# Three staging buffers for a float64 weight conversion, with router operands formed per 128 features

## The chip, the cores and the metric

The program runs on one core of one Trainium2 chip. The metric is the device time of one execution in microseconds (us). Inputs lie in device memory (HBM); the host only re-lays them, without arithmetic. The core has five engines with an in-order queue each: TensorE (PE in the profile, its weight loads PEld), VectorE (DVE), ScalarE (ACT), GpSimd (POOL), and SyncE (SP), which here issues all DMA transfers. An instruction that waits holds up everything behind it on its engine.

## The reference

Three stages in a row on 2304 tokens (4 batches of 576), width 512:

```python
scores = scale * q @ k.T + (cum[:, None] - cum[None, :])   # cum = cumsum(log f); causal
x = softmax(scores) @ v                                     # 8 heads of 64
x = (silu(x @ w_gate) * (x @ w_val)) @ w_out                # d_ff 1536; these weights are float64
P = exp(x @ moe2_w_gate - max)                              # 8 experts, dense
for _ in range(8): P /= P.sum(1); P /= P.sum(0); P *= N / E # balanced over rows and columns
out = sum_e P[:, e] * (relu(x @ w1[e]) @ w2[e])             # 8 experts, inner size 1024
```

The three weights of the middle stage are float64: numpy's draw is scaled by a float64 scalar. The kernel gets them as raw 64-bit words and makes float32 values of them on the chip. All large products are done on a high and a low part of each operand (float32r), three matmuls for one.

## The kernel before, in words

The work is four "units", one for a batch. Unit b is attention of batch b (`attn_unit`, eight heads in four pairs) and the gated feed-forward of batch b (`moe_unit`, six slices of 256 inner features, each in two token blocks of 288). `merge` interleaves attention of batch b+1 with the feed-forward of batch b in program order; a scheduler of the tile framework, which models the engines, then sets each engine's order of instructions. After the fourth unit the second phase starts: the router's balancing and the eight experts.

The float64 weights come in 18 pieces of 1 MB, three for a slice: two of the up-projections, one of the down-projection. `convert(i)` turns piece i into a float32 high and low part:

- SyncE loads the raw words into a tile `st` (line 103). Two such tiles exist, so the load of piece i+2 stands on SyncE's queue behind the end of piece i.
- VectorE masks the exponent word (line 111, into `y`), ScalarE shifts it (113, `y` to `g`), VectorE sets the sign (114), masks (116, into `y` again) and scales the middle word (117, in place in `st`).
- GpSimd adds the two in two halves (122, in `st`). ScalarE copies each half into the high part of a tile `w` (124) and GpSimd forms the low part by `rest` (line 143, a helper: `out = src - hi`).
- SyncE stores `w` to HBM (`wsplit`, 126), whence units 1 to 3 fetch it again (`fetch`, 138).

The `w` tiles are a ring of four. Unit 0 multiplies directly from it, so a piece is written to its `w` only when unit 0 has used up the piece four before it. Line 151 (helper `three`) is every three-part matmul of the feed-forward and of the down-projections of the experts: tile `pm` for the up-projections, `py` for the down-projections. Per slice that is 96 `pm` and 48 `py` matmuls of 288 columns in a unit, 144 for three pieces.

In attention, `qk` and `cb` are the loads of a head (232, 244), `qkh` and `kl` the split by GpSimd. For batches 2 and 3 a masked copy `cm` of `cb` takes the tiles of tag `st`.

At a unit's end `finish` (from line 446) stores the result `x` and forms the router's products: for each half of the tokens, `x` is split into high and low parts (tile `f`, 128x576 at a time, line 456 on ScalarE, `rest` on GpSimd), multiplied into a PSUM tile `pl` (460; one of three tiles that `pm` and `py` use too), copied to `ls` (464) and stored to `lgd` (465). Pool `frm` holds two `f` tiles and one `ls`.

Of the kernel before, what the change touches and what calls it, by code (L numbers as in the profile page):

```python
# [8 lines left out]
F32 = mybir.dt.float32  # L9
F32R = mybir.dt.float32r  # L10
BF16 = mybir.dt.bfloat16
U16 = mybir.dt.uint16
U32 = mybir.dt.uint32
AF = mybir.ActivationFunctionType
ALU = mybir.AluOpType
# [18 lines left out]
def attention_two_ffns(ctx: ExitStack, tc: tile.TileContext, qkT, vt, f, wf, g2, w1, w2, out):  # L34
    nc = tc.nc
    B, H, D, _, S = qkT.shape
# [4 lines left out]
    P = 128  # L41
    KD = DM // P
# [4 lines left out]
    HP = 512  # L47
# [13 lines left out]
    frm = m_ctx.enter_context(pool("frm", 2))  # L61
# [15 lines left out]
    gw = const.tile([P, KD, P], F32R, name="gw")  # L77
# [5 lines left out]
    HB = S // 2  # L83
# [14 lines left out]
    def convert(i):  # L98
        base = bases[:, 1:2] if i % 3 == 2 else bases[:, 0:1]
        W = 2 * HP  # L100
        st = cvp.tile([P, 4 * W + 4], U16, tag="st", name="st", bufs=2)
        with tc.issue_after(last_qk[0].ins) if i < PACE else ExitStack():
            nc.sync.dma_start(out=st[:, 1:1 + 4 * W], in_=wf[i].bitcast(U16))

        def words(dt):
            return st.bitcast(dt)[:, 0:2 * W].rearrange("p (i t) -> p i t", t=2)[:, :, 1]
        mid, v = words(U32), words(F32)
        top = st[:, 4:4 + 4 * W].rearrange("p (i t) -> p i t", t=4)[:, :, 0]
        y = cvp.tile([P, W], U16, tag="y", name="y")
        g = cvp.tile([P, W], U16, tag="g", name="g")  # L110
        nc.vector.tensor_scalar(out=y, in0=top, scalar1=0x7fff, scalar2=None, op0=ALU.bitwise_and)  # L111

        nc.scalar.activation(out=g, in_=y, func=AF.Relu, scale=8.0, bias=base)
        nc.vector.scalar_tensor_tensor(
            out=g, in0=top, scalar=0x8000, in1=g, op0=ALU.bitwise_and, op1=ALU.bitwise_or)
        nc.vector.tensor_scalar(out=y, in0=g, scalar1=0xff80, scalar2=None, op0=ALU.bitwise_and)
        nc.vector.scalar_tensor_tensor(
            out=v, in0=mid, scalar=2.0**-36, in1=y.bitcast(BF16), op0=ALU.mult, op1=ALU.mult)
        t = wring.tile([P, 2, 2, HP], F32R, tag="w", name="w")
        halves = [slice(j * HP, (j + 1) * HP) for j in range(2)]  # L120
        for h in halves:
            nc.gpsimd.tensor_tensor(out=v[:, h], in0=v[:, h], in1=g[:, h].bitcast(BF16), op=ALU.add)  # L122
        for j, h in enumerate(halves):
            nc.scalar.copy(out=t[:, j, 0], in_=v[:, h])  # L124
            rest(t[:, j, 1], v[:, h], t[:, j, 0])
        nc.sync.dma_start(out=wsplit[i], in_=t.bitcast(F32))
        return t
# [13 lines left out]
    def rest(out, src, hi, eng=None):  # L141

        (eng or nc.gpsimd).tensor_tensor(out=out, in0=src, in1=hi.bitcast(F32), op=ALU.subtract)  # L143
# [13 lines left out]
    cvp = at_ctx.enter_context(pool("cvp", 2, side="right"))  # L157
# [47 lines left out]
    def attn_unit(b):  # L205
# [22 lines left out]
        def load(h):  # L228
            qk = raw.tile([P, 2, S], F32, tag="qk", name="qk")
            src = qkT[b, h]  # L230
# [4 lines left out]
            if r < NPE:  # L235

                for c0 in (0, HB):
                    ps = ps_t.tile([P, 512], F32, tag="t", name="ps_c")
                    nc.tensor.matmul(
                        out=ps[:, 0:HB], lhsT=ident[0:B * H, r:r + 1].to_broadcast([B * H, P]), rhs=ct[:, c0:c0 + HB],  # L240
                        start=True, stop=True)
# [2 lines left out]
                nc.sync.dma_start(out=cb, in_=cumd[r:r + 1, :].to_broadcast([P, S]))  # L244
            cm = None
            if b in MASKED:
                cm = cvp.tile([P, 8 * HP + 4], U16, tag="st", name="cm", bufs=2).bitcast(F32)[:, 0:S]
                nc.gpsimd.tensor_tensor(
                    out=cm[:, 0:512].rearrange("p (t c) -> p t c", c=P), in0=cb[:, 0:512].rearrange("p (t c) -> p t c", c=P),
                    in1=maskf.unsqueeze(1).to_broadcast([P, 4, P]), op=ALU.add)  # L250
                nc.gpsimd.tensor_tensor(out=cm[64:P, 512:S], in0=cb[64:P, 512:S], in1=maskf[64:P, 64:P], op=ALU.add)
# [143 lines left out]
    def moe_unit(b, get=fetch, ready=None):  # L395
# [50 lines left out]
        def finish():  # L446

            x = xa["x"]
            nc.sync.dma_start(out=xd[b], in_=x)
            for j in range(2):  # L450
                tk = slice(j * HB, (j + 1) * HB)
                pl = ps_m.tile([P, 512], F32, tag="m", name="pl")
                for i in range(2):
                    t = frm.tile([P, 2, 2, HB], F32R, tag="f", name="f")
                    src = x[:, 2 * i:2 * i + 2, tk]
                    nc.scalar.copy(out=t[:, 0], in_=src)
                    rest(t[:, 1], src, t[:, 0])
                    ops = [(hl, k) for k in range(2) for hl in range(2)]
                    for n, (hl, k) in enumerate(ops):
                        nc.tensor.matmul(  # L460
                            out=pl[:, 0:HB], lhsT=gw[:, 2 * i + k], rhs=t[:, hl, k],
                            start=(i == 0 and n == 0), stop=(i == 1 and n == len(ops) - 1))
                ls = frm.tile([P, HB], F32, tag="ls", name="ls", bufs=1)
                nc.scalar.copy(out=ls[0:2 * E], in_=pl[0:2 * E, 0:HB])
                nc.sync.dma_start(out=lgd[:, b * S + j * HB:b * S + (j + 1) * HB], in_=ls[0:2 * E])

# [301 lines left out]
```

## Time and profile before

| | |
|---|---|
| runs, median of 3 (lowest to highest) | 2263.25 us (2262.04 to 2266.35) |
| the profiled execution | 2262.41 us |
| its span, first to last instruction | 2260.6 us |
| TensorE busy | 2210.3 us, 98% |
| VectorE, GpSimd, ScalarE busy | 75%, 40%, 38% |
| moved from and to HBM | 193.27 MB read, 36.87 MB written |

A busy share is a mean over stages that differ: conversion runs only in the first 282.4 us, the experts from some 740 us on. So the rows below look at stretches. A "window" row gives for a stretch each engine's busy time and its number of instructions; the stretch's length stands in front. In the "chain of waits" each piece is what released the next, back from the last instruction.

### The profile page before, as it was taken

How to read it: one execution, taken by the hardware profiler on the slowest of the kernel's cores; microseconds unless marked ns; L12 is line 12 of the kernel's file. 1: busy time of each engine (PE TensorE's matmuls, PEld its weight loads, DVE VectorE, ACT ScalarE, POOL GpSimd, SP SyncE). 2: the span in 40 equal slices, each digit the busy share in tenths (PEclk: the TensorE clock that was granted, in tenths of full speed). 3: DMA queues.
4: the chain of work that ended last, by engine and by line, in shares of the span. 5: the costliest groups of instructions: out<-in, count | busy, mean ns of one | idle time of the engine just before them, and what ended most of it. 6: DMA issues, size and time to landing. Idle time of an engine off the chain costs nothing.

```text
span 2260.6 us, 36388 instructions
## 1 busy us (share of the span) xinstructions
PE 2210.3 (98%) x13801; PEld 2013.9 (89%) x13801; DVE 1698.7 (75%) x3513; ACT 852.6 (38%) x1952; POOL 908.8 (40%) x716
## 2 busy tenths in 40 slices
PE   7898799999999999999999999999999999999999
PEld 5698799999999888898898989988989898988997
DVE  7778755656635798887878878877788887887876
ACT  7866464555422434322323223233232232322321
POOL 6869754544523454332323323233232332322320
PEclk9999999999999999999999999999999999999999
DMA  9766566554544332111111111151111111111101
GB/s 251 203 204 218 197 206 194 188 187 149 206 160 154 102 118 87 63 47 38 56 38 47 47 38 53 60 211 54 38 48 47 38 57 38 47 47 38 57 29 52
DMA packets 105103, 232.50 MB, mean 103 GB/s; under 512 B 10672, under 2 KB 60128, under 8 KB 92896
## 3 DMA queue, kind: packets, MB, share of 16 engines
q1 hardware_dynamic: 104928, 230.18, 31.5%
q8 instruction: 108, 1.77, 0.3%
q14 instruction: 67, 0.55, 0.1%
HBM read 193.27 MB, written 36.87 MB: 102 GB/s over the span
## 4 chain that ended last, share of the span: by engine, by line
PE 84%; DMA 6%; DVE 4%; POOL 2%; ACT 1%; issue 1%; SPq 1%; POOLq 0%; DVEq 0%; ACTq 0%
PE py L151 40%; PE pa L614 30%; PE pm L151 10%; DMA st<-wf 3%; PE ps_o L353 2%; PE ps_t L322 1%; DMA rd<-rt 1%; PE ps_s L279 1%; PE ps_s L283 1%; DVE al L629 1%; DMA rb<-rd 1%; DMA qk<-qkT 1%; DVE y L111 0%; DVE sm L580 0%; POOL st L122 0%
## 5 line engine op out<-in xcount | busy, mean ns | idle before, releaser
L614 PE MATMUL pa<-xf,w1h 128*128 128x288 f32 x3584 | 748.7, 295 | 0.2 <-DVE u L623 0.2
L614 PEld LDWEIGHTS pa<-xf,w1h 128*128 128x128 f32 x3584 | 597.6, 188 | 37.8 <-DVE u L623 0.7
L666 DVE SCALAR_TENSOR_TENSOR acc<-py,lg,acc 128x512 f32<-128x512 f32 x531 | 394.8, 744 | 246.6 <-PE py L151 246.4
L614 PE MATMUL pa<-xf,w1l 128*128 128x288 f32 x1792 | 527.6, 295 | 0.0
L143 POOL TENSOR_TENSOR w2l<-w,w2h 128x1024 fp32r<-128x1024 f32 x64 | 154.7, 2418 | 819.2 <-ACT w2h L590 819.2
L151 PE MATMUL py<-w2h,ah 128*128 128x512 f32 x1152 | 454.2, 394 | 1.8 <-DVE acc L659 0.7
L151 PE MATMUL py<-w2l,ah 128*128 128x512 f32 x1152 | 454.0, 394 | 0.0
L151 PE MATMUL py<-w2h,al 128*128 128x512 f32 x1152 | 453.3, 393 | 0.0
L629 DVE SCALAR_TENSOR_TENSOR al<-c,ah 128x288 fp32r<-128x288 f32 x512 | 429.7, 866 | 5.6 <-ACT ah L628 4.9
L628 ACT ACTIVATE ah<-c 128x288 fp32r<-128x288 f32 x512 | 208.2, 443 | 566.3 <-PE py L151 319.0
L614 PEld LDWEIGHTS pa<-xf,w1l 128*128 128x128 f32 x1792 | 337.0, 188 | 10.6
L151 PE MATMUL pm<-xh,w 128*128 128x288 f32 x1536 | 331.2, 300 | 13.6 <-ACT w L124 8.9
L151 PEld LDWEIGHTS pm<-xh,w 128*128 128x128 f32 x1536 | 255.0, 190 | 17.8 <-ACT w L124 10.6
L151 PEld LDWEIGHTS py<-w2h,al 128*128 128x128 f32 x1152 | 216.3, 188 | 50.0
L151 PEld LDWEIGHTS py<-w2h,ah 128*128 128x128 f32 x1152 | 216.3, 188 | 31.0 <-DVE acc L666 2.3
L151 PEld LDWEIGHTS py<-w2l,ah 128*128 128x128 f32 x1152 | 216.3, 188 | 26.2
L151 PE MATMUL pm<-xl,w 128*128 128x288 f32 x768 | 228.0, 297 | 0.5 <-POOL xl L143 0.5
L634 ACT COPY m<-pa 128x288 f32<-128x288 f32 x128 | 50.3, 393 | 435.8 <-PE pa L614 433.6
L143 POOL TENSOR_TENSOR w1l<-w,w1h 128x256 fp32r<-128x256 f32 x192 | 162.2, 872 | 128.7 <-ACT w1h L586 128.7
L151 PE MATMUL py<-ah,w 128*128 128x288 f32 x768 | 174.4, 299 | 4.5 <-DVE xa L444 2.1
L143 POOL TENSOR_TENSOR w1l<-sm,w1h 128x1024 fp32r<-128x1024 f32 x64 | 153.8, 2403 | 2.5 <-ACT w1h L586 2.5
L143 POOL TENSOR_TENSOR al<-th,ah 128x288 fp32r<-128x288 f32 x96 | 82.9, 866 | 160.6 <-ACT ah L428 157.9
(149 smaller groups left out, 3099.4 us busy)
## 6 DMA issues: line engine op xcount, KB each, us to landing
w<-w SPq DMA_DIRECT2D x128, 512.0 KB, 3.6
w<-wsplit SPq DMA_DIRECT2D x54, 1024.0 KB, 5.0
qk<-qkT SPq DMA_DIRECT2D x64, 288.0 KB, 7.1
st<-wf SPq DMA_DIRECT2D x18, 1024.0 KB, 9.8
wsplit<-w SPq DMA_DIRECT2D x18, 1024.0 KB, 4.5
cb<-cumd SPq DMA_DIRECT2D x31, 288.0 KB, 6.1
xo<-h SPq DMA_DIRECT2D x28, 288.0 KB, 2.2
xf<-xo SPq DMA_DIRECT2D x14, 576.0 KB, 11.0
```

What stands on the lines that cost most here:

```text
L143: (eng or nc.gpsimd).tensor_tensor(out=out, in0=src, in1=hi.bitcast(F32), op=ALU.subtract)
L151: nc.tensor.matmul(out=ps, lhsT=a, rhs=b, start=(i == 0), stop=(i == n - 1))
L279: nc.tensor.matmul(out=ps[:, 0:w], lhsT=a[:, qs:qs + P], rhs=kh[:, c0:c0 + w], start=True, stop=False)
L283: nc.tensor.matmul(out=ps[:, 0:w], lhsT=a[:, qs:qs + P], rhs=kl[:, c0:c0 + w], start=False, stop=True)
L322: nc.tensor.transpose(pv[:, j, :], pt[r0:P, k0:k0 + P], ident[r0:P, r0:P])
L353: nc.tensor.matmul(out=po[:, c0:w], lhsT=vs[:, j, e].rearrange("p a d -> p (a d)"), rhs=pts[rng][part][:, j, c0:w], start=(i == 0), stop=( ...
L614: nc.tensor.matmul(out=ps, lhsT=w[:, MW[m - 1], k], rhs=x[:, m - 1, hl, k], start=(n == 0), stop=(n == len(ops) - 1))
L628: nc.scalar.activation(out=ah[:, f, tk], in_=src, func=AF.Relu)
L629: nc.vector.scalar_tensor_tensor(out=al[:, f, tk], in0=src, scalar=0.0, in1=ah[:, f, tk].bitcast(F32), op0=ALU.max, op1=ALU.subtract)
L634: nc.scalar.copy(out=m1, in_=p1)
L666: nc.vector.scalar_tensor_tensor(out=a, in0=py, scalar=lg[:, t, e:e + 1], in1=a, op0=ALU.mult, op1=ALU.add)
```

## The change

The tag `st` gets a third buffer (at both places that use it). The masked exponent word is written to `g` instead of `y`, and ScalarE works on `g` in place; `y` keeps one buffer, `g` gets three. The router operands are formed per 128 features (eight tiles of 128x288 in high and low part for a batch's two halves) instead of per 256; `ls` takes a tile of the same tag `f`, so that `f` and `ls` share two buffers.

```diff
--- before.py
+++ after.py
@@ -98,7 +98,7 @@
     def convert(i):
         base = bases[:, 1:2] if i % 3 == 2 else bases[:, 0:1]
         W = 2 * HP
-        st = cvp.tile([P, 4 * W + 4], U16, tag="st", name="st", bufs=2)
+        st = cvp.tile([P, 4 * W + 4], U16, tag="st", name="st", bufs=3)
         with tc.issue_after(last_qk[0].ins) if i < PACE else ExitStack():
             nc.sync.dma_start(out=st[:, 1:1 + 4 * W], in_=wf[i].bitcast(U16))
 
@@ -106,11 +106,11 @@
             return st.bitcast(dt)[:, 0:2 * W].rearrange("p (i t) -> p i t", t=2)[:, :, 1]
         mid, v = words(U32), words(F32)
         top = st[:, 4:4 + 4 * W].rearrange("p (i t) -> p i t", t=4)[:, :, 0]
-        y = cvp.tile([P, W], U16, tag="y", name="y")
-        g = cvp.tile([P, W], U16, tag="g", name="g")
-        nc.vector.tensor_scalar(out=y, in0=top, scalar1=0x7fff, scalar2=None, op0=ALU.bitwise_and)
-
-        nc.scalar.activation(out=g, in_=y, func=AF.Relu, scale=8.0, bias=base)
+        y = cvp.tile([P, W], U16, tag="y", name="y", bufs=1)
+        g = cvp.tile([P, W], U16, tag="g", name="g", bufs=3)
+        nc.vector.tensor_scalar(out=g, in0=top, scalar1=0x7fff, scalar2=None, op0=ALU.bitwise_and)
+
+        nc.scalar.activation(out=g, in_=g, func=AF.Relu, scale=8.0, bias=base)
         nc.vector.scalar_tensor_tensor(
             out=g, in0=top, scalar=0x8000, in1=g, op0=ALU.bitwise_and, op1=ALU.bitwise_or)
         nc.vector.tensor_scalar(out=y, in0=g, scalar1=0xff80, scalar2=None, op0=ALU.bitwise_and)
@@ -244,7 +244,7 @@
                 nc.sync.dma_start(out=cb, in_=cumd[r:r + 1, :].to_broadcast([P, S]))
             cm = None
             if b in MASKED:
-                cm = cvp.tile([P, 8 * HP + 4], U16, tag="st", name="cm", bufs=2).bitcast(F32)[:, 0:S]
+                cm = cvp.tile([P, 8 * HP + 4], U16, tag="st", name="cm", bufs=3).bitcast(F32)[:, 0:S]
                 nc.gpsimd.tensor_tensor(
                     out=cm[:, 0:512].rearrange("p (t c) -> p t c", c=P), in0=cb[:, 0:512].rearrange("p (t c) -> p t c", c=P),
                     in1=maskf.unsqueeze(1).to_broadcast([P, 4, P]), op=ALU.add)
@@ -450,17 +450,15 @@
             for j in range(2):
                 tk = slice(j * HB, (j + 1) * HB)
                 pl = ps_m.tile([P, 512], F32, tag="m", name="pl")
-                for i in range(2):
-                    t = frm.tile([P, 2, 2, HB], F32R, tag="f", name="f")
-                    src = x[:, 2 * i:2 * i + 2, tk]
-                    nc.scalar.copy(out=t[:, 0], in_=src)
-                    rest(t[:, 1], src, t[:, 0])
-                    ops = [(hl, k) for k in range(2) for hl in range(2)]
-                    for n, (hl, k) in enumerate(ops):
+                for k in range(KD):
+                    t = frm.tile([P, 2, HB], F32R, tag="f", name="f")
+                    nc.scalar.copy(out=t[:, 0], in_=x[:, k, tk])
+                    rest(t[:, 1], x[:, k, tk], t[:, 0])
+                    for hl in range(2):
                         nc.tensor.matmul(
-                            out=pl[:, 0:HB], lhsT=gw[:, 2 * i + k], rhs=t[:, hl, k],
-                            start=(i == 0 and n == 0), stop=(i == 1 and n == len(ops) - 1))
-                ls = frm.tile([P, HB], F32, tag="ls", name="ls", bufs=1)
+                            out=pl[:, 0:HB], lhsT=gw[:, k], rhs=t[:, hl],
+                            start=(k == 0 and hl == 0), stop=(k == KD - 1 and hl == 1))
+                ls = frm.tile([P, 2, HB], F32, tag="f", name="ls")[:, 0]
                 nc.scalar.copy(out=ls[0:2 * E], in_=pl[0:2 * E, 0:HB])
                 nc.sync.dma_start(out=lgd[:, b * S + j * HB:b * S + (j + 1) * HB], in_=ls[0:2 * E])
 
```

The scheduler makes a new order of the whole program from it. On SyncE's queue near its start (names: `st_507`, `st_776`, `st_1062` are pieces 1, 2 and 3; `cb` and `qk` loads of heads; `wsplit0` the store of piece 0), before:

```order
L103 DMA st_507<-wf 128x4096
L244 DMA cb_421<-cumd_166 128x576
L232 DMA qk_524<-qkT 64x1152 x2
L232 DMA qk_626<-qkT 64x1152
L244 DMA cb_527<-cumd_166 128x576
L232 DMA qk_626<-qkT 64x1152
L126 DMA wsplit0_112<-w_233 128x2048
L103 DMA st_776<-wf 128x4096
L232 DMA qk_715<-qkT 64x1152 x2
```

and now:

```order
L103 DMA st_507<-wf 128x4096
L103 DMA st_776<-wf 128x4096
L244 DMA cb_421<-cumd_166 128x576
L232 DMA qk_524<-qkT 64x1152 x2
L232 DMA qk_626<-qkT 64x1152
L244 DMA cb_527<-cumd_166 128x576
L232 DMA qk_626<-qkT 64x1152
L126 DMA wsplit0_112<-w_233 128x2048
L103 DMA st_1062<-wf 128x4096
```

The load of piece 2 has moved up past `cb` and `qk` loads of three heads and past the store of piece 0, to the place right behind the load of piece 1; the load of piece 3 now stands behind the store of piece 0.

In the middle of the conversion the same queue had, before (`st_1838` and `st_1855` are pieces 9 and 10, `rd` and `rb` the normalisation of a pair of heads):

```order
L126 DMA wsplit7_119<-w_1458 128x2048
L103 DMA st_1838<-wf 128x4096
L305 DMA rd1_1_182<-rt_2190 10x128
L310 DMA rb_2193<-rd1_1_182 64x512
L311 DMA rb_2193<-rd1_1_182 64x64
L310 DMA rb_2193<-rd1_1_182 64x512
L311 DMA rb_2193<-rd1_1_182 64x64
L126 DMA wsplit8_120<-w_1475 128x2048
L103 DMA st_1855<-wf 128x4096
```

and now (`st_1872` is piece 11):

```order
L126 DMA wsplit7_119<-w_1458 128x2048
L103 DMA st_1855<-wf 128x4096
L244 DMA cb_2923<-cumd_166 128x576
L126 DMA wsplit8_120<-w_1475 128x2048
L103 DMA st_1872<-wf 128x4096
```

Behind the store of piece 7 stands now the load of piece 10 instead of piece 9, behind that of piece 8 the load of piece 11 instead of 10.

On ScalarE at the end of unit 2 (`f` the router operand's copy, `th` and `ah` of the next unit's feed-forward, `xf` an operand of the second phase), before:

```order
L456 CAST f_7718<-xa_5603 128x576
L456 CAST f_7729<-xa_5603 128x576
L464 COPY ls_7725<-pl_7710 16x288
L456 CAST f_7736<-xa_5603 128x576
L425 ACTIVATE th_7827<-pm_7801 128x288
L522 CAST xf_7779<-xst_7780 128x2x288
L522 CAST xf_7779<-xst_7780 128x288
L428 CAST ah_7799<-th_7827 128x288
L522 CAST xf_7779<-xt_7782 128x4x288
L425 ACTIVATE th_7859<-pm_7833 128x288
L428 CAST ah_7799<-th_7859 128x288
L464 COPY ls_7743<-pl_7728 16x288
```

and now:

```order
L462 COPY ls_7755<-pl_7734 16x288
L455 CAST f_7759<-xa_5627 128x288
L425 ACTIVATE th_7863<-pm_7837 128x288
L455 CAST f_7764<-xa_5627 128x288
L428 CAST ah_7835<-th_7863 128x288
L455 CAST f_7769<-xa_5627 128x288
L425 ACTIVATE th_7895<-pm_7869 128x288
L455 CAST f_7774<-xa_5627 128x288
L428 CAST ah_7835<-th_7895 128x288
L425 ACTIVATE th_7929<-pm_7903 128x288
L462 COPY ls_7779<-pl_7758 16x288
```

After the first `ls` stood one copy of `f` and then the feed-forward; now four stand there, each in front of a `th` or `ah`.

## Rows read from the trace of the kernel before

**Rows 1.** The page: busy time of the engines; chain of waits by line.
```profile
PE 2210.3 (98%) x13801; PEld 2013.9 (89%) x13801; DVE 1698.7 (75%) x3513; ACT 852.6 (38%) x1952; POOL 908.8 (40%) x716
...
PE py L151 40%; PE pa L614 30%; PE pm L151 10%; DMA st<-wf 3%; PE ps_o L353 2%; PE ps_t L322 1%; DMA rd<-rt 1%; PE ps_s L279 1%; PE ps_s L283 1%; DVE al L629 1%; DMA rb<-rd 1%; DMA qk<-qkT 1%; DVE y L111 0%; DVE sm L580 0%; POOL st L122 0%
```

**Rows 2.** Windows over stretches: each engine's busy us (count), clock, DMA share, GB/s.
```profile
core 0: us, PE busy (x) PEld busy (x) DVE busy (x) ACT busy (x) POOL busy (x), PEclk, DMA share, GB/s
0.00:60.00 60.00, 44.04 (x233) 31.55 (x233) 44.75 (x117) 44.61 (x104) 38.68 (x35) 1.00 0.89 245
120.00:220.00 100.00, 94.42 (x698) 88.71 (x697) 77.67 (x163) 66.18 (x151) 80.31 (x66) 1.00 0.65 212
180.00:220.00 40.00, 36.46 (x264) 33.34 (x263) 34.18 (x72) 29.23 (x66) 34.90 (x28) 1.00 0.70 223
220.00:280.00 60.00, 46.54 (x299) 42.77 (x298) 43.43 (x77) 26.11 (x51) 47.10 (x39) 0.91 0.57 202
260.00:274.00 14.00, 10.74 (x47) 10.10 (x48) 8.19 (x9) 5.06 (x8) 10.69 (x9) 0.63 0.53 198
300.00:740.00 440.00, 438.25 (x3300) 431.28 (x3299) 237.42 (x700) 202.09 (x495) 196.23 (x188) 1.00 0.53 178
```

**Rows 3.** Chain of waits, 120 to 290 us (start, length): loads of pieces.
```profile
150.53 9.82 DMA st<-wf
...
176.09 8.82 DMA st<-wf
...
253.27 6.88 DMA st<-wf
```

**Rows 4.** SyncE's queue in order of time: stores and loads of pieces.
```profile
191.21 0.33 SPq L126 DMA_DIRECT2D wsplit<-w  x1
191.59 0.42 SPq L103 DMA_DIRECT2D st<-wf  x1
...
205.11 0.42 SPq L103 DMA_DIRECT2D st<-wf  x1
...
262.99 0.37 SPq L103 DMA_DIRECT2D st<-wf  x1
...
282.40 0.32 SPq L126 DMA_DIRECT2D wsplit<-w  x1
```

**Rows 5.** Instructions on tile st: ns min/median/max, first and last start.
```profile
L122 POOL TENSOR_TENSOR st<-st,g x36: 1143/1176/1737, 20.5 to 278.6; 128x512 f32<-128x512 f32 x36
...
L143 POOL TENSOR_TENSOR w<-st,w x36: 1288/1316/2305, 25.7 to 281.0; 128x512 fp32r<-128x512 f32 x36
```

**Rows 6.** Waits from 120 to 290 us: who for whom, us, times, longest.
```profile
DVE y L111 <- DMA st<-wf: 12.4, 7, 3.4
...
PE pm L151 <- ACT w L124: 8.9, 7, 3.1
```

**Rows 7.** Waits from 0 to 120 us.
```profile
DVE y L111 <- DMA st<-wf: 13.5, 4, 5.8
```

**Rows 8.** Line 143 on GpSimd from 120 to 280 us.
```profile
L143 POOL TENSOR_TENSOR al<-th,ah x21: 789/812/1782, 119.5 to 276.3; 128x288 fp32r<-128x288 f32 x21
```

**Rows 9.** DMA issues: KB each, median us to landing.
```profile
qk<-qkT SPq DMA_DIRECT2D x64, 288.0 KB, 7.1
st<-wf SPq DMA_DIRECT2D x18, 1024.0 KB, 9.8
...
xo<-h SPq DMA_DIRECT2D x28, 288.0 KB, 2.2
...
lgd<-ls SPq DMA_DIRECT2D x8, 18.0 KB, 3.3
```

**Rows 10.** Instructions on the router's tile f.
```profile
L456 ACT CAST f<-xa x16: 663/674/677, 289.9 to 735.6; 128x576 fp32r<-128x576 f32 x16
L143 POOL TENSOR_TENSOR f<-xa,f x16: 1412/1433/1647, 294.0 to 736.9; 128x576 fp32r<-128x576 f32 x16
```

**Rows 11.** Window at the router's step of unit 2.
```profile
610.00:620.00 10.00, 9.72 (x74) 9.49 (x73) 5.73 (x9) 4.03 (x8) 7.63 (x6) 1.00 0.93 311
```

## The prediction

> **What bounds the kernel now.** I read first the page, then windows over stretches, then, inside the stretch that stands out, the chain of waits, SyncE's queue and the waits.
>
> The page shows TensorE at 98% and three of its matmul lines as 80% of the chain of waits; the loads of float64 pieces are 3% [rows 1]. The windows say where something is to be had [rows 2]. From 300 to 740 us TensorE is busy 438.25 of 440 us: nothing that shortens a wait there can pay. In the first 60 us it is idle 15.96 us, in 120 to 220 us 5.58 us, in 220 to 280 us 13.46 us. The last stretch also has a low clock: from 260 to 274 us, just after TensorE's longest idle time, the granted clock is 0.63, so it stood at 1.2 instead of 2.4 GHz most of the time, and over the 60 us the mean is 0.91, which is 60 x 0.09 = 5.4 us of lost matmul time. So between 120 and 280 us at most 5.58 + 13.46 + 5.4 = 24.4 us can be won, and since TensorE is full from 280 us on and its work is the same in both kernels, what is won there stays won.
>
> What ends last in that stretch is the conversion. Three loads of pieces stand on the chain of waits with 9.82, 8.82 and 6.88 us, 25.5 us in all [rows 3]. On SyncE's queue a load goes out 0.38 us after the store of the piece two before it (191.21, 191.59): it has waited for its buffer, and only then does its transfer begin [rows 4]. From 205.11 to 262.99 us five pieces take 57.88 us, 11.58 us each, while the last needs 282.40 - 262.99 = 19.41 us from the issue of its load to its store. Two in flight at 19.4 us each cannot do better than 9.7 us a piece. TensorE waits for such pieces 8.9 us by name (`pm` for the copy to `w`) [rows 6].
>
> **The change, part by part.** The sum is made against the profiled execution, 2262.41 us, which is 0.84 us under the median of 2263.25.
>
> *A. The third `st`.* The load of piece i+3 now stands behind the store of piece i, as the order shows, so a transfer of some 9 us runs while two other pieces are worked on, and VectorE's waits for it (12.4 us in this stretch) go [rows 6]. Three in flight allow 19.41 / 3 = 6.5 us a piece. What is late next? TensorE needs 144 / 3 = 48 matmuls a piece at 438.25 / 3300 = 0.133 us, 6.4 us. GpSimd needs 2 x 1.176 + 2 x 1.316 = 4.98 us for the piece [rows 5] and for the feed-forward four `al` a slice, 4 x 0.812 / 3 = 1.08 us [rows 8]: 6.1 us, before any work of attention. The two are nearly equal, and GpSimd has more: 80.31 + 47.10 = 127.41 us of work in these 160 us [rows 2]. It cannot be full, since ScalarE's and VectorE's steps stand between its own; the best it did in the stretch's busiest window is 34.90 of 40 us, 0.87. At that share the same work takes 127.41 / 0.87 = 146 us, a gain of 14 us. The bounds are 0, if GpSimd's share stays at 127.41 / 160 = 0.80, and 24.4 us. I take 14.
>
> *B. The earlier loads.* The load of piece 2 now goes ahead of `cb` and `qk` loads of three heads, and one more piece is loaded before attention of batch 0 is through. In the first 60 us the DMA engines are busy 0.89 at 245 GB/s [rows 2], so 1 MB takes 1.05 / 0.245 = 4.3 us of the time of all engines, and everything behind it comes that much later. That a load waits in line there is seen from its landing: 7.1 us for the 288 KB of `qk`, 2.2 us for the 288 KB of a store `xo` in a quiet stretch [rows 9]. VectorE's mask of the piece stands in front of attention's reductions and waits for the load; that cost 13.5 us of idle VectorE before 120 us [rows 7]. The cost lies between -4 us (the earlier loads end less than a third of those waits and lose nothing) and 2 x 4.3 = 8.6 us (two loads ahead, nothing hides them). I take 3 us, less than one load, as heads have two buffers.
>
> The Trainium skill, "DMA: Bandwidth & Descriptors", section "Queues, rings and completion order", has a rule for this that speaks against the change: on each DMA engine the descriptors of a queue are consumed in ring order, so small loads cannot overtake the 1 MB in front of them. The 7.1 us beside 2.2 us agree. By the rule alone B would be the full 4.3 us and the sum 1.3 us higher.
>
> *C. The router's operands.* Per unit 8 copies of 128x288 instead of 4 of 128x576 on ScalarE (0.674 us each before; at most 4 x 0.674 = 2.7 us more) and 8 GpSimd differences at 0.812 instead of 4 at 1.433 [rows 8, 10]: 6.50 - 5.73 = 0.77 us more. Neither engine is full there: 4.03 and 7.63 of 10 us at unit 2 [rows 11]. The matmuls are the same. What is new is a wait: `ls` takes one of two buffers, so the second `f` of the second half waits for the landing of `lgd` (3.3 us [rows 9]), and a `th` or `ah` of the next slice stands behind it on ScalarE. `pl` also keeps one of three PSUM tiles longer. TensorE lost 0.28 us in the window of unit 2's step [rows 11]. Cost: between 0 and 3.3 us a unit, 0 to 13 us for four; a stall of 3.3 us is about as long as the two groups of matmuls that TensorE has in hand (24 x 0.133 = 3.2 us), so I take 0.4 us a unit, 1.5 us.
>
> *D. The rest.* ScalarE's step in place and VectorE's mask into `g` are as many instructions of the same size: 0. The single `y` is written and read by VectorE alone, in its order, so it makes no wait. The third buffer for `cm` falls into units 2 and 3, where TensorE is full: 0. The new order of everything else moves what I cannot price; 2 us either way.
>
> Sum: 2262.41 - 14 + 3 + 1.5 = 2252.9, forecast 2253 us.
>
> **The rivals.**
>
> *No gain, 0.25.* GpSimd was the bound already, and its share does not rise: pieces come earlier into `st` and lie there, since the ring of four `w` tiles, not `st`, lets them out. For it: the ring is unchanged, and 4.98 us a piece are GpSimd's. Against: from 220 to 280 us GpSimd is idle 12.9 of 60 us [rows 2], while loads go out only behind stores. A would be 0 to 8 us, say 4: 2262.4 - 4 + 4.5 = 2263 us.
>
> A page makes this likelier: the Trainium skill, "GPSIMD Engine Reference", section "8. Key points", says that GpSimd shares its SBUF interfaces with VectorE and contends with VectorE's instructions that have two SBUF inputs or a two-port mode. The difference to `w`, 1.288 us at the least and 2.305 at the most for one shape [rows 5], agrees. More overlap of pieces would bring more such long ones.
>
> *Slower, 0.13.* Attention of batch 0 sets the start of unit 0, and it is behind the earlier pieces: two loads of 4.3 us ahead of its heads, and the masks, which VectorE takes in order, in front of its reductions for as long. B is then 8.6 us plus some 5 us more of VectorE's waits, A only 5 us since TensorE's demand comes later and pieces pile up: 2262.4 - 5 + 13.6 + 1.5 = 2272 us. It decides from the point at which B is larger than A. Against it: a head's loads have two buffers, and what is converted early need not be converted later.
>
> *A full gain, part of the forecast's case.* GpSimd has the pieces ready in time, idle time and low clock both go: A near 24 us, B and C small, 2262.4 - 24 + 3 = 2241 us.
>
> **How the numbers follow.** Forecast's case 0.62, no gain 0.25, slower 0.13. The forecast's own range is 2241 to 2259. The range for 8 in 10 goes from 2241 up to 2267, past the case of no gain and its 4 us of unpriced order; it leaves out most of the slower case. A run of this kernel can tell 0.2%, 4.5 us, from no change: faster means below 2258.7 us, slower above 2267.8. Nearly all of the forecast's case is under it, a tenth of it is not, and some of the case of no gain is: faster 0.60, same 0.27, slower 0.13.
>
> **What would show it.** A: from 120 us on the loads go out ahead of need and land before VectorE's mask, so that VectorE no longer waits for `st`; the last store of a piece comes some 10 us before 282.4 us; the window of what was 220 to 280 us shows TensorE busier, GpSimd at 0.87 and no low clock. It is wrong if the last store comes as late as before, or if GpSimd's share is as it was. B: attention of batch 0 ends (last `xl` of unit 0) some 3 us later than before. C: a wait of ScalarE's `f` for the landing of `lgd`, and TensorE's idle time at the router's steps under 1 us each. What would prove the forecast wrong as a whole is TensorE idle after 300 us that was not there: then the new order, not the buffers, made the time.

## The result, and the profile after

The change makes the kernel slower: 2278.74 us (2273.31 to 2291.69, 6 runs) against 2263.89 us for the kernel before (6 runs), a ratio of 1.0071 with a 95% interval of 1.0056 to 1.0087. The forecast was 2253 us, in a range that ended at 2267.

The profiled execution took 2278.44 us. On its page, the busy time of the engines and the chain of waits by line:

```profile
PE 2219.6 (97%) x13801; PEld 2019.6 (89%) x13801; DVE 1697.7 (75%) x3513; ACT 852.7 (37%) x1968; POOL 926.6 (41%) x732
...
PE py L151 38%; PE pa L612 29%; PE pm L151 10%; PE ps_o L353 1%; PE ps_t L322 1%; DMA xo<-h 1%; DVE al L627 1%; DMA xst<-xd 1%; DMA lgd<-ls 1%; PE ps_s L279 1%; PE ps_s L283 1%; DVE c L621 0%; POOL h L143 0%; DVE xt L534 0%; DVE sm L578 0%
```

The loads of pieces (`st<-wf`, 3% in [rows 1]) are gone from this list; new in it are `xst<-xd` and `lgd<-ls`, two transfers at a unit's end, and `xo<-h`, a store of the second phase. The windows over the stretches of [rows 2] and [rows 11], in the same columns:

```profile
0.00:60.00 60.00, 43.41 (x225) 31.78 (x226) 46.62 (x114) 46.03 (x106) 43.50 (x36) 0.97 0.91 262
120.00:220.00 100.00, 92.22 (x670) 86.78 (x670) 86.35 (x175) 67.45 (x153) 89.71 (x67) 0.98 0.72 244
180.00:220.00 40.00, 35.71 (x256) 34.02 (x256) 34.88 (x66) 24.87 (x52) 39.02 (x30) 0.96 0.79 260
220.00:280.00 60.00, 56.35 (x408) 54.39 (x407) 43.51 (x106) 31.41 (x73) 51.03 (x42) 0.97 0.63 204
260.00:274.00 14.00, 14.00 (x106) 13.54 (x105) 8.79 (x31) 9.01 (x22) 11.58 (x12) 1.00 0.94 297
300.00:740.00 440.00, 429.19 (x3166) 419.63 (x3165) 220.57 (x631) 183.91 (x456) 181.96 (x185) 0.98 0.49 167
610.00:620.00 10.00, 7.45 (x29) 7.11 (x30) 0.95 (x2) 2.60 (x5) 5.89 (x6) 0.52 0.33 134
```

From 220 to 280 us TensorE does 408 matmuls instead of 299, and the clock of 260 to 274 us is full instead of 0.63. From 300 to 740 us it does 3166 instead of 3300; at 0.133 us each these 134 matmuls are 17.8 us, an estimate of what is lost there. The rest of the loss comes behind 740 us. The window at unit 2's router step shows the worst of it: 29 matmuls in 10 us, at a clock of 0.52, so at 1.2 instead of 2.4 GHz nearly all the time.

The conversion by itself went as it was meant to. SyncE's queue with the last stores of pieces, and VectorE's wait for `st` from 120 to 290 us (who for whom, us, times, longest):

```profile
229.27 0.42 SPq L103 DMA_DIRECT2D st<-wf  x1
244.08 0.32 SPq L126 DMA_DIRECT2D wsplit<-w  x1
247.61 0.34 SPq L126 DMA_DIRECT2D wsplit<-w  x1
259.57 0.33 SPq L126 DMA_DIRECT2D wsplit<-w  x1
```

```profile
DVE g L111 <- DMA st<-wf: 5.2, 3, 2.5
```

The last load goes out at 229.27 instead of 262.99 us, the last store at 259.57 instead of 282.40 [rows 4], and 5.2 us of the 12.4 us of waiting are left [rows 6]. Unit 0 starts its down-projections earlier, as the first and last start in the tile view of `py` up to 300 us show, first before, then after:

```profile
L151 PE MATMUL py<-ah,w x192: 288/294/445, 124.8 to 296.3; 128*128 128x288 f32 x192
```

```profile
L151 PE MATMUL py<-ah,w x192: 288/294/432, 117.3 to 279.8; 128*128 128x288 f32 x192
```

At its start the lead is 7.5 us, at its end 16.5 us. Then it is lost. The table follows it, with one profiled execution of each kernel: the start of the last `py` of each unit, of the 109th `py` matmul of the second phase (796.3 us before) and of the last, minus the same start in the kernel before (us; the edits of e1 to e12 are below).

| kernel | unit 0 | unit 1 | unit 2 | unit 3 | 796 us | end |
|---|---|---|---|---|---|---|
| after | -16.5 | -6.1 | -5.6 | +3.4 | +7.8 | +16.0 |
| e1 narrow router alone | -1.0 | +7.2 | +6.3 | +16.6 | +22.1 | +30.3 |
| e6 narrow, two `f`, own `ls` | +1.8 | +8.8 | +6.7 | +12.9 | +14.6 | +18.8 |
| e7 narrow, four `f`, own `ls` | -0.5 | -0.8 | -0.4 | 0.0 | +0.5 | +0.8 |
| e3 conversion words alone | -2.1 | -2.4 | -2.8 | -2.6 | -2.6 | -2.0 |
| e2 third `st`, old router | +3.4 | +6.7 | +4.6 | +8.1 | +17.1 | +22.0 |
| e4 after, `ls` in the ring of `th` | -15.1 | +4.5 | +0.7 | +11.7 | +24.5 | +29.1 |
| e5 after, wide in `ah`, `al` | -12.1 | -10.2 | -12.3 | -7.9 | -1.3 | +3.5 |
| e9 after, unit 3 wide | -14.6 | -4.8 | -2.0 | +7.2 | +7.4 | +15.4 |
| e8 after, all wide | -15.6 | -13.7 | -15.6 | -9.4 | -9.2 | -2.6 |
| e10 as e8, two `st` | -1.0 | -0.9 | +0.8 | +3.3 | +3.5 | +8.0 |
| e11 as e8, no 1e-9 | -15.3 | -13.4 | -15.4 | -10.8 | -10.6 | -6.2 |
| e12 before, no 1e-9 | +1.4 | +1.1 | +1.4 | +1.9 | +2.0 | +1.6 |

The lead falls in steps: 10.4 us between the ends of units 0 and 1, 9.0 us between those of units 2 and 3, 4.4 us to 796 us and 8.2 us from there to the end. The first step is order in part: between these two marks the kernel after does 1242 matmuls and the kernel before 1197, and the 45 more are 6.0 us at 0.133 us each; between the next two marks it does 55 fewer. The first three steps lie around the router's products, the last one does not.

The tile view of `pl`, then TensorE's waits from 275 to 760 us (who for whom, us, times, longest), first before:

```profile
L460 PE MATMUL pl<-f,gw x64: 291/295/399, 297.1 to 741.3; 128*128 128x288 f32 x64
...
PE pl L460 <- ACT f L456: 0.3, 1, 0.3
```

and after:

```profile
L458 PE MATMUL pl<-f,gw x64: 290/296/609, 280.1 to 749.0; 128*128 128x288 f32 x64
...
PE pl L458 <- ACT f L455: 3.3, 3, 2.2
PE pa L612 <- ACT xf L520: 3.0, 2, 1.9
...
PE pl L458 <- POOL f L143: 1.9, 4, 0.5
```

TensorE's idle time for `f` grows from 0.3 us to 5.2 us, 3.0 us more are for `xf`, and the slowest matmul goes from 399 to 609 ns, as some run at the low clock. At unit 2 the timeline of the kernel after shows how (start, length; in brackets the idle time before and what ended it). TensorE's waiting rows, then ScalarE's and GpSimd's of the same stretch:

```profile
607.79 0.40 PE L612 MATMUL pa<-xf,w1h 128*128 128x288 f32 x1 [1.03 <-ACT xf L520]
...
611.74 1.33 PE L612 MATMUL pa<-xf,w1h 128*128 128x288 f32 x4 [1.94 <-ACT xf L520]
615.08 0.61 PE L458 MATMUL pl<-f,gw 128*128 128x288 f32 x1 [0.81 <-ACT f L455]
```

```profile
601.96 0.43 ACT L455 CAST f<-xa 128x288 fp32r<-128x288 f32 x1 [0.36 <-DVE xa L444]
607.06 1.00 ACT L520 CAST xf<-xst 128x576 fp32r<-128x576 f32 x2 [4.67 <-DMA xst<-xd]
607.97 0.76 ACT L455 CAST f<-xa 128x288 fp32r<-128x288 f32 x2
610.53 1.15 ACT L520 CAST xf<-xt 128x1152 fp32r<-128x1152 f32 x1 [1.80 <-DVE xt L516]
```

```profile
607.81 2.38 POOL L143 TENSOR_TENSOR xf<-xst,xf 128x576 fp32r<-128x576 f32 x2 [4.53 <-ACT xf L520]
610.15 1.75 POOL L143 TENSOR_TENSOR f<-xa,f 128x288 fp32r<-128x288 f32 x2
```

ScalarE stands 4.67 us at a copy for the second phase, for a transfer. Two copies of `f`, the second at 601.96 us, are all that two narrow tiles let it make ahead; the third and fourth (607.97 us) stand in its order behind that `xf`, the fifth behind the next `xf`, which waits again. GpSimd does `xf` before `f` for the same reason. TensorE does a few matmuls here and there, and its clock falls. Before, two wide tiles held four such copies: all four wide copies of the unit (607.49 to 613.24 us) stand ahead of the first `xf` (615.42 us).

TensorE's own order differs too, and most of its idle time here is not for `f`. From 600 to 630 us it waits 3.4 us for `xf`, in front of `pa`, a product of the second phase, and 1.1 us for `f`. The scheduler put the first `pa` at 607.8 us, among the `pl` that begin at 606.1 us; before, it comes at 617.4 us, when the last `pl` of the unit has started (617.3 us).

At units 1 and 3 it is also the transfer of `ls`. At unit 1 an `f` waits 4.68 us for it, the longest such wait, and TensorE stands 2.2 us for that `f`. At unit 3 the ScalarE timeline shows:

```profile
742.04 0.39 ACT L462 COPY ls<-pl 16x288 f32<-16x288 f32 x1
742.33 0.43 ACT L455 CAST f<-xa 128x288 fp32r<-128x288 f32 x1
745.62 0.43 ACT L455 CAST f<-xa 128x288 fp32r<-128x288 f32 x1 [2.86 <-DMA lgd<-ls]
...
749.36 1.00 ACT L584 CAST w1h<-w 128x256 fp32r<-128x256 f32 x3
```

The second `f` of the second half waits 2.86 us for `ls` to leave, and the first operand of an expert's weights (`w1h`) comes behind it at 749.36 us (before: 739.96 us). TensorE had other matmuls during these 2.86 us; it then stands 1.4 us in three waits for GpSimd's part of the last `f`.

### The profile page after: what moved, and what is told of

Its sections match the earlier page's. It is cut to its first block, busy times and chain, and to the rows that moved or that the text cites. A ratio compares the mean times of both kernels' runs of the same rounds, so it can differ in the third digit from the quotient of the medians.

```text
span 2276.5 us, 36408 instructions
## 1 busy us (share of the span) xinstructions
PE 2219.6 (97%) x13801; PEld 2019.6 (89%) x13801; DVE 1697.7 (75%) x3513; ACT 852.7 (37%) x1968; POOL 926.6 (41%) x732
## 4 chain that ended last, share of the span: by engine, by line
PE 81%; DVE 3%; DMA 3%; issue 1%; ACT 1%; POOL 1%; SPq 0%; POOLq 0%; ACTq 0%; DVEq 0%
PE py L151 38%; PE pa L612 29%; PE pm L151 10%; PE ps_o L353 1%; PE ps_t L322 1%; DMA xo<-h 1%; DVE al L627 1%; DMA xst<-xd 1%; DMA lgd<-ls 1%; PE ps_s L279 1%; PE ps_s L283 1%; DVE c L621 0%; POOL h L143 0%; DVE xt L534 0%; DVE sm L578 0%
## 5 line engine op out<-in xcount | busy, mean ns | idle before, releaser
L627 DVE SCALAR_TENSOR_TENSOR al<-c,ah 128x288 fp32r<-128x288 f32 x512 | 423.4, 855 | 7.7 <-ACT ah L626 7.2
```

The source lines that it names most:

```text
L627: nc.vector.scalar_tensor_tensor(out=al[:, f, tk], in0=src, scalar=0.0, in1=ah[:, f, tk].bitcast(F32), op0=ALU.max, op1=ALU.subtract)
```

## The experiments

Theory R: the router's operands cost it, and the third `st` is a gain. Rival O: the scheduler's new order costs it, whatever edit made it; further rivals are named in the expectations. The first three take the change apart.

**e1: the router's part alone**, on the kernel before.

```diff
+                for k in range(KD):
+                    t = frm.tile([P, 2, HB], F32R, tag="f", name="f")
...
-                ls = frm.tile([P, HB], F32, tag="ls", name="ls", bufs=1)
+                ls = frm.tile([P, 2, HB], F32, tag="f", name="ls")[:, 0]
```

> The kernel before with only the router operands per 128 features and ls in their two buffers; conversion as before (two st, two y, two g). Theory R (the narrower router step costs the time: at unit ends 0 to 3 it holds ScalarE, GpSimd and a PSUM tile longer, and at the phase switch it delays the first expert weights): the loss of some 30 us that the traces show behind unit 0, without the 16 us that the third st buffer wins: 2285 to 2300 us. Theory O (any edit gives a new scheduled order, and that order, above all the early place of the second phase's operands at the end of unit 2, costs the time; the router step costs the 1.5 us of the prediction): 2260 to 2270 us.

2295.73 us, ratio 1.0132 (1.0115 to 1.0149). By the table it is level with the kernel before up to the end of unit 0, where its first router step is, and loses 31 us from there on, as theory R expected; the rest of the change gives back 17 us of it. The order is new here too, so this run alone doesn't part the operands from the order made for them.

**e2: the rest alone**, with other places for what the old router needs.

```diff
+        st = cvp.tile([P, 4 * W + 4], U16, tag="st", name="st", bufs=3)
+        nc.vector.tensor_scalar(out=low(U16), in0=g, scalar1=0xff80, scalar2=None, op0=ALU.bitwise_and)
...
+                ls = tmp.tile([P, 288], F32, tag="th", name="ls")
```

> The third st buffer with the router step as before (two f tiles of 256 features). Its space comes from elsewhere: the masked word goes into the unused low words of st instead of y, g has two buffers, ls lies in a buffer of th, ones is allocated in the second phase. Theory R: the gain of the third buffer is kept, 2245 to 2255 us. Theory O: the order is new again and costs as in the changed kernel, 2270 to 2285 us.

2282.47 us, 1.0081 (1.0069 to 1.0093). This is the range of theory O. It lost the gain in the conversion (+3.4 us at unit 0), 9.0 us between the end of unit 3 and 796 us, and 4.9 us behind. Four things were exchanged for room at once, so it settles nothing; e8 does what it was to do.

**e3: the conversion's words alone** (`y` once, `g` three times), on the kernel before.

```diff
+        y = cvp.tile([P, W], U16, tag="y", name="y", bufs=1)
+        g = cvp.tile([P, W], U16, tag="g", name="g", bufs=3)
+        nc.scalar.activation(out=g, in_=g, func=AF.Relu, scale=8.0, bias=base)
```

> The kernel before with only the conversion words turned in one tile (mask into g, ScalarE in place, one y, three g). Theory R: no cost and no gain, 2260 to 2268 us. Theory O: a new order as any, so up to 15 us away from before on either side.

2264.48 us, 1.0002 (0.9991 to 1.0014): nothing. This new order of the program costs nothing, which speaks against O as a rule for any edit; e10 below shows an order that does cost.

**e4: the kernel after, `ls` in the ring of `th`.**

```diff
-                ls = frm.tile([P, 2, HB], F32, tag="f", name="ls")[:, 0]
+                ls = tmp.tile([P, 288], F32, tag="th", name="ls")
```

> The changed kernel with ls in a buffer of th instead of f, so that the two f buffers are for f alone and no f waits for the landing of lgd. Theory R with the wait for lgd as its main part: at least half of the 30 us comes back, 2255 to 2265 us. Theory R with two narrow buffers as the main part: 2273 to 2282 us. Theory O: a new order again, anywhere from 2255 to 2285 us.

2293.8 us, 1.0133 (1.0118 to 1.0148), slower still and above every range. From 275 to 820 us `th` waits for the transfer only 0.5 us; TensorE's longest wait is 4.9 us at the switch to the second phase, for the load of the router's products from `lgd`. Why that load comes late is not shown, so the run doesn't decide between the two parts of theory R.

**e5: the kernel after with 256-feature operands**, as tiles of the rings `ah` and `al`; `ls` has its own.

```diff
+                    hi = actp.tile([P, 2, 288], F32R, tag="ah", name="fh")
+                    lo = actp.tile([P, 2, 288], F32R, tag="al", name="fl")
...
+                ls = frm.tile([P, HB], F32, tag="ls", name="ls", bufs=1)
```

> The changed kernel (third st, words in one tile) with the router operands per 256 features again, high part in a buffer of ah and low part in one of al (the feed-forward's own rings of two), ls in a buffer of its own. Theory R (the narrower router step costs some 30 us, the third buffer wins some 16): 2245 to 2256 us, unit 0 ending some 16 us earlier than before and the lead kept to the end. Theory O (the new order behind unit 0 costs it, whatever the router's width): 2270 to 2290 us.

2266.83 us, 1.0012 (1.0004 to 1.0021), 12 us under the kernel after, between the ranges. The lead holds to the end of unit 2; then 4.4 us are lost to the end of unit 3, 6.6 us at the switch and 4.8 us behind. No run shows why.

**e6 and e7: what in the narrow operands costs.** Both are the kernel before with narrow operands and `ls` apart; e6 has two `f` tiles, e7 four, as many bytes as two wide ones.

```diff
-                    t = frm.tile([P, 2, HB], F32R, tag="f", name="f")
+                    t = frm.tile([P, 2, HB], F32R, tag="f", name="f", bufs=4)
```

> The kernel before with router operands per 128 features in two buffers, but ls in a buffer of its own as before. Against the kernel with ls in f's buffers (2295.7 us). If the shared ring is the cause (an f waits for the landing of lgd): 2264 to 2272 us. If two narrow operands in flight are (each half as much data, one round trip ScalarE, GpSimd, TensorE per 128 features): 2285 to 2296 us.

> The kernel before with router operands per 128 features in four buffers and ls in its own: the same space and the same data in flight as before, but twice the instructions on ScalarE and GpSimd. If the depth of f (two narrow buffers) or the shared ring is the cause: 2262 to 2270 us. If the number of steps is: 2280 to 2296 us.

e6: 2283.15 us, 1.0084 (1.007 to 1.0099). e7: 2265.6 us, 1.0009 (1.0001 to 1.0018). The windows from 600 to 630 us, of e1, e6 and e7 in this order:

```profile
600.00:630.00 30.00, 24.09 (x143) 22.86 (x143) 11.78 (x24) 7.11 (x15) 12.96 (x13) 0.83 0.57 209
```

```profile
600.00:630.00 30.00, 26.33 (x180) 25.09 (x179) 11.63 (x23) 8.14 (x18) 14.40 (x14) 0.94 0.57 207
```

```profile
600.00:630.00 30.00, 29.96 (x221) 29.23 (x220) 12.77 (x28) 11.25 (x26) 18.44 (x19) 1.00 0.76 263
```

With four tiles TensorE is full; with two it is idle 3.67 us and loses clock; with `ls` among the two, 5.91 us. So the eight narrow steps are nearly free (2 us by the median). Two tiles instead of four cost 2283.15 - 2265.6 = 17.6 us, which is just under the range for two narrow operands in flight, and `ls` in the ring 2295.73 - 2283.15 = 12.6 us more.

These are prices of a ring together with the order that the scheduler makes for it. TensorE's waits of e6 from 600 to 630 us are nearly all for `xf`:

```profile
PE pa L612 <- ACT xf L520: 2.9, 2, 1.9
PE pa L612 <- POOL xf L143: 0.4, 1, 0.4
PE pl L458 <- ACT f L455: 0.3, 1, 0.3
```

As in the kernel after, the first `pa` of e6 stands just behind the first `pl` of unit 2 (620.0 and 618.3 us); in e7 it stands at their end (616.5 us, the last `pl` at 616.8). And by the table some 4 us of the 17.6 arise behind 796 us, where no `f` is formed any more. No run has two narrow tiles in the order of e7, so what the depth costs without the order is not shown.

**e8, e9 and e10: wide operands where there is room.** e8 is the kernel after with wide operands everywhere: units 0 to 2 as in e5, unit 3 in a pool of its own, opened in space that is free by then. e9 does so for unit 3 alone. e10 is e8 with two `st`.

```diff
+                if b == B - 1:
+                    for i in range(2):
+                        t = frm3[0].tile([P, 2, 2, HB], F32R, tag="f", name="f", bufs=2)
...
+    frm3.append(f3_ctx.enter_context(pool2("frm3", 1, side="right")))
```

> The changed kernel with router operands of 256 features everywhere: in ah and al for units 0 to 2, and for unit 3 in a pool of its own with two wide f and one ls as before. Theory R (the narrow router step eats the gain, at the unit ends and at the switch to the second phase): the lead of 12 to 16 us at the end of unit 0 is kept, 2246 to 2256 us, faster than before. Theory S (the first 160 us of the second phase have a limit of their own, VectorE with the balancing, which gives back what comes earlier): 2262 to 2268 us.

> The changed kernel, narrow operands in units 0 to 2, but for unit 3 two wide f and one ls in a pool of their own. Theory R: the 3 us behind at the end of unit 3 stay, the 12 us lost at the switch go: 2263 to 2269 us. Theory S: the 12 us are lost anyway, 2274 to 2281 us.

> As e8 but with two st buffers: unit 0 ends as before, no lead. Both theories: 2260 to 2268 us. The difference to e8 is what the third st is worth at the end of the program: 12 to 16 us by theory R, 0 to 4 by theory S.

e8: 2261.54 us, 0.9992 (0.9983 to 1.0001). e9: 2277.65 us, 1.0059 (1.0047 to 1.0071). e10: 2274.64 us, 1.0047 (1.0034 to 1.0059). Between e10 and e8 only the third `st` differs: 14.6 us at the end of unit 0 and 13.1 us at the median. That is theory R's 12 to 16 us, not theory S's 0 to 4: between these two the lead is kept. But e8 as a whole, between the two theories' ranges, is no faster than the kernel before, and e10, without any lead, is 10.3 us slower (ratio 1.0047) and above both theories' range. So wide operands in these places cost some 10 us by themselves, with the order that comes with them; no run parts the two. e9 came out as theory S had it: the switch costs 0.2 us instead of 4.4, yet 8.0 us are lost behind it.

e8 carries its lead through the switch (-9.2 us), then loses 6.6 us between 796 us and the end; e9 and e10 lose 8.0 and 4.5 us there, and e6, with no third `st`, 4.2. Most of it falls before 910 us, into the balancing of the router's weights: from 796 to 910 us TensorE is idle 6.0 us in e8 and 2.2 us before. In e8 VectorE's timeline there is

```profile
831.64 0.29 DVE L719 TENSOR_REDUCE rs<-lg 128x18 f32<-128x144 f32 x1
833.00 1.90 DVE L551 TENSOR_TENSOR xt<-xst 128x288 f32<-128x288 f32 x2 [1.07 <-POOL h L143]
834.82 0.99 DVE L647 SCALAR_TENSOR_TENSOR al<-c,ah 128x288 fp32r<-128x288 f32 x1
835.74 2.31 DVE L720 TENSOR_SCALAR rs<-rs 128x18 f32<-128x18 f32 x1
837.96 0.68 DVE L677 TENSOR_TENSOR acc<-py,acc 128x512 f32<-128x512 f32 x1
```

beside GpSimd's, and TensorE's next row:

```profile
832.93 2.56 POOL L143 TENSOR_TENSOR w1l<-w,w1h 128x256 fp32r<-128x256 f32 x3
835.45 2.56 POOL L143 TENSOR_TENSOR w1l<-sm,w1h 128x1024 fp32r<-128x1024 f32 x1
```

```profile
838.69 0.50 PE L151 MATMUL py<-w2h,ah 128*128 128x512 f32 x1 [3.11 <-DVE acc L677]
```

An addition to 18 numbers a partition lasts 2.31 us, to 838.05 us; GpSimd's long difference ends at 838.01 us. Behind it on VectorE is `acc`, for which TensorE waits 3.11 us. The tile view of `rs` from 780 to 910 us shows what the same instruction takes otherwise (ns, lowest, median, highest), before and in e8:

```profile
L702 DVE TENSOR_SCALAR rs<-rs x8: 160/333/773, 783.8 to 860.7; 128x18 f32<-128x18 f32 x8
```

```profile
L720 DVE TENSOR_SCALAR rs<-rs x7: 163/178/2307, 784.9 to 858.5; 128x18 f32<-128x18 f32 x7
```

The last of these in e8 was held too, for which no matmul waited:

```profile
858.51 2.11 DVE L720 TENSOR_SCALAR rs<-rs 128x18 f32<-128x18 f32 x1
```

```profile
858.20 2.38 POOL L143 TENSOR_TENSOR w1l<-sm,w1h 128x1024 fp32r<-128x1024 f32 x1
```

Of the eight in e8, five had no GpSimd instruction beside them and took 163 to 178 ns; three had one and ended 0.03 to 0.04 us after it (239, 2307 and 2111 ns). In the kernel before, three alone took 160 to 168 ns and five beside a shorter GpSimd instruction 324 to 773 ns, each ending 0.03 to 0.04 us after it.

**e11 and e12: without that instruction**, in e8 and, as a control, in the kernel before. Both leave out the addition of 1e-9 to the row sums.

```diff
-            nc.vector.tensor_scalar_add(out=rs, in0=rs, scalar1=1e-9)
```

> Third st with wide router operands, as in the run called all wide, but it leaves out the addition of 1e-9 to the row sums in the balancing (8 VectorE instructions of 128x18). There one of the eight took 2.31 us instead of 0.18 us, from 835.74 to 838.05 us, while GpSimd worked on a 128x1024 difference from 835.45 to 838.01 us, and TensorE then stood 3.11 us for VectorE's acc behind it. Theory G (that VectorE instruction is held until GpSimd's long one ends, and this costs the 3 us): the idle 3.11 us goes, the lead of 9.2 us at 790 us is kept to -6 or better at the end, time some 3 to 6 us under all wide's 2261.5: 2256 to 2259, ratio to before near 0.997. Rival O2 (any order that the scheduler finds here loses some 6 us): the wait turns up at another instruction of VectorE, and the time stays at 2261 to 2264, ratio 0.999 to 1.000.

> Control: the kernel before, without the same eight additions of 1e-9. In its trace they last 0.16 to 0.77 us and nothing stands behind them. Theory G: no change beyond the new order, 2261 to 2266, ratio 0.999 to 1.001. If the eight instructions or their place in a chain cost time by themselves, it gains as much as the other run does, 3 to 6 us, ratio 0.997 to 0.998; then the other run's gain says nothing on G.

e11: 2258.51 us, 0.9967 (0.9954 to 0.998), the only one whose interval lies under the kernel before. e12: 2264.07 us, 0.9996 (0.9984 to 1.0007). Who waited on TensorE from 800 to 910 us, e8 and then e11 (us, times, longest):

```profile
PE py L151 <- DVE acc L677: 4.3, 3, 3.1
```

```profile
PE py L151 <- DVE acc L677: 2.2, 2, 1.2
...
PE pa L632 <- DVE c L641: 1.3, 1, 1.3
```

The long wait is gone and the control stands still, so theory G holds for this wait. It is not all: e11 still loses 4.4 us of its lead there (10.6 to 6.2), and 1.4 us of its gain over e8 was there before 796 us, which is within the spread of one kernel's executions.

## Why the prediction was wrong, point by point

- **A, the third `st`: the number came out, in part by luck.** Predicted -14 us, bounds 0 to -24.4, for the stretch from 120 to 280 us. Measured at the end of unit 0: -14.6 us (e10 to e8); at the median -13.1 us (e10 to e8) and -17.0 us (e1 to after). But the third `st` brings B with it, and A and B together were put at -11. Of the lead 7.5 us are there before 120 us, in a stretch from which the sum expected a loss; from there to unit 0's end, the stretch of A, it is 9.0 us. GpSimd, named as the next limit, is busy 39.02 of 40 us from 180 to 220 us; I had put its best at 0.87. That it is the limit there is read from this share and not tested. Nor is the share all work, as the rivals below show.
- **B, the earlier loads: wrong in sign.** Predicted +3 us, with the last `xl` of unit 0 some 3 us later. GpSimd's four `xl` of unit 0, before and after:

```profile
L143 POOL TENSOR_TENSOR xl<-bt,xh x4: 1415/1512/1857, 57.7 to 110.0; 128x576 fp32r<-128x576 f32 x4
```

```profile
L143 POOL TENSOR_TENSOR xl<-bt,xh x4: 1413/1420/1870, 62.2 to 102.5; 128x576 fp32r<-128x576 f32 x4
```

  The delay is there for the first pair of heads, 4.5 us, and the first `pm` comes 1.9 us later (78.41 instead of 76.55 us). By the last pair it has turned into a lead of 7.5 us, which the first `py` has as well. VectorE waits 4.6 us for a piece up to 120 us, not 13.5 [rows 7]; the earlier loads ended most of those waits, where the lower bound of B gave them a third. The early loads move 262 instead of 245 GB/s in the first 60 us. The landing times say little: the 7.1 us for `qk` [rows 9] is the median of the 7 loads of 64 whose landing the trace has, and 7.2 us after is that of 8. The ring order that the Trainium skill states ("DMA: Bandwidth & Descriptors", section "Queues, rings and completion order") is the order in which descriptors are consumed; the same section says that a later one may finish its write before an earlier one, so "cannot overtake" is more than it states. The late first pair is what such an order would give, but no run here tests it.
- **C, the router's operands: the step that failed.** It stood in the sum at 1.5 us, with bounds of 0 and 13; e1 measures 31 us at the end of the kernel. Its working counted instructions and engines' free time, and that was right (e7: 2 us). It priced the wait for `lgd` per unit and took TensorE's two groups of matmuls in hand as cover; the wait came as named (8.5 us in three waits over the kernel), but the cover held only in part: at unit 1 a wait of 4.68 us left TensorE idle for 2.2 us, at unit 3 one of 2.86 us was covered. `ls` in the ring costs 12.6 us by e6 against e1. What the step left out is that two wide tiles had become two narrow ones, half the data on the way from ScalarE over GpSimd to TensorE: 17.6 us by e7 against e6. The order made for such a ring puts `f` behind an `xf` that waits for a transfer, and `pa` among the `pl`; TensorE then stands for `xf` and `f`, and behind that idle time the clock falls, as in [rows 2] at 260 us. How much of the 17.6 us is the depth itself and how much the order stays open.
- **D, the rest: right for the words, too small for the order.** e3 measures nothing. But new orders were put at 2 us either way, and e10 loses 10.3 us with neither a third `st` nor narrow operands.
- **"What is won there stays won": it held between like kernels, but not its reason.** From e10 to e8, 14.6 us at the end of unit 0 are 13.1 us at the median; from e1 to after, 15.5 us are 17.0. Against the kernel before, e8 keeps 15.6 us to unit 2's end, 9.2 us to the switch, 2.6 us to the end; but e10 falls 8.0 us back on the same way without a lead, so that is mostly a cost of the variant. The reason given was that TensorE is full from 280 us on. That was so in the kernel before; in the kernel after it is idle 10.81 us from 300 to 740 us, not 1.75, and in the balancing, too, what engines do at the same moment decides.
- **The rivals.** No gain (0.25): its A of 0 to 8 us is not far from the 9.0 us of A's own stretch, and more of GpSimd's differences did become long, as the rival said. The tile view of `st` after, beside [rows 5]:

```profile
L143 POOL TENSOR_TENSOR w<-st,w x36: 1294/1477/2309, 25.8 to 258.2; 128x512 fp32r<-128x512 f32 x36
```

  Its median is 1477 instead of 1316 ns, and with the additions in `st` the conversion's GpSimd instructions take 108.4 instead of 96.4 us in all. So GpSimd's share of 120 to 220 us rose from 0.80 to 0.90, but in part by longer instructions, where the sum took the work as the same. Where the rival was wrong is that pieces, though longer on GpSimd, were done sooner.

  Slower (0.13): right in sign, its 2272 us near the measured 2278.74 by luck, wrong in mechanism, since B was a gain in the end. The last test of the prediction, TensorE idle after 300 us, came true, but "the new order, not the buffers, made the time" is half wrong: it was buffers, those of the router, with the order made for them.

Three things stay open: depth or order in C; what in the balancing takes e11's remaining 4.4 us; and why the variants with wide operands and a third `st` (e5, e8, e11) lose 4 to 6 us between the ends of units 2 and 3.

## What to carry to other kernels

Count a ring by the data that it keeps in flight, not by its number of buffers: here halving the tile and keeping two of them cost 17.6 us, with the order that the scheduler made for it, while four halves cost 2 us. A tile that a transfer holds should not share a ring with tiles on the way to the busiest engine. Room for a new buffer is best sought where it is not live at the same time: unit 3's own pool took the loss at the switch from 4.4 us (after) to 0.2 us (e9), though little of that was left at the end.

A gain in an early stage can be kept and still not show, as from e10 to e8, because what made room for it costs as much elsewhere. So measure it against a kernel with the same other changes, and look again at every later stage with two or three engines in step.

## What the runs showed of the hardware

A small VectorE instruction from SBUF to SBUF can be held until a GpSimd instruction ends: 2.31 us instead of 0.18 us for 128x18, ending 0.04 us after GpSimd's. It was 2307 ns in e8 and did the same in two more orders (2307 ns in e9, 2306 in e10), and shorter ones were held in the kernel before. The Trainium skill ("SBUF — State Buffer", section "Who interferes with whom") says that VectorE and GpSimd share one pair of ports and that it is an exclusive lock; the trace agrees. So the price of such an instruction can be that of the GpSimd one beside it, not its own size.

After its idle stretches at unit 2 TensorE was granted 0.52 of full speed from 610 to 620 us, in a stage in which the kernel before ran at 1.00 [rows 11]. At the 0.133 us a matmul of full speed its 7.45 busy us would be 56 matmuls; it did 29. So of the 45 matmuls missing against 74, some 18 go to idle time and 27 to the clock, by this estimate: in that window the lost clock cost more than the waits, though no single wait there was longer than 1.94 us.
